# Seven block products for all six token blocks: the second MLP's first product in a fused attention and two-MLP kernel

## The chip, the cores and the metric

The kernel runs on one core of a Trainium2 chip. The metric is the device time of one execution in microseconds (us). Three runs of the kernel before took 1200.7, 1200.85 and 1199.98 us; their median is 1200.7 us.

## The reference

Three layers follow each other on 3072 tokens of 512 values. Attention runs over chunks of 32 tokens with 16 tokens of context to the left, 8 to the right and 8 memory tokens. The first MLP has a width of 1536, the second one of 2048. The change lies in the second:

```python
def _moe2_ref(x, w_in, w_out):
    h = x @ w_in                                  # 3072 x 512 times 512 x 2048
    g = h * (1.0 / (1.0 + np.exp(-1.702 * h)))
    return (g @ w_out).astype(np.float32)         # 3072 x 2048 times 2048 x 512
```

All inputs are 64-bit floats in DRAM. The kernel turns each weight block of 128 x 512 into two tiles of 32-bit floats, a high part and a low part (the rest), and it makes one product of two such numbers out of three matmuls: high by high, high by low, low by high.

## The kernel before

**Order of the work.** The code does not write instructions directly. Every step is handed to `add(engine, cost, function, reads, writes)` of the class `Schedule`. At the end `run` goes through the steps with the estimated costs and starts on each engine the ready step with the earliest due time. The due times come from TensorE's products, whose sum of costs is the variable `clock[0]`. What comes out is one fixed list per engine (TensorE or PE, VectorE or DVE, ScalarE or ACT, GpSimd or POOL, and SyncE or SP, which issues DMAs). On the chip each engine goes through its list in order, and an instruction that waits holds all those behind it on its engine.

**First MLP.** The tokens are six blocks of 512. For each block, `first_product` makes 12 column blocks of each of the two inner products (12 matmuls of 128x512 for each, 8 on line 740 and 4 on line 747). `gated` makes the gate: ScalarE's tanh on line 764, VectorE's product on line 767, then the high part on ScalarE (line 772) and the low part on VectorE (line 775). `gemm2` adds the outer product into the four banks Y (line 918). The result of a block is copied out of Y by ScalarE (line 938) and stored in DRAM as `y_dram`, transposed.

**Conversion of weights.** `convert` loads a block of 64-bit floats into one of three tiles `raw` (line 254) and turns it into 32-bit floats in one of two tiles `f`: ScalarE shifts the exponent (line 258), VectorE shifts the low words (line 263), VectorE (line 272) or, every second time, ScalarE (line 268) isolates the sign, and VectorE joins the parts (line 277). Then ScalarE writes the high part into a weight slot (line 282), and VectorE, or every third time GpSimd, writes the low part (line 287). The 16 blocks of `w2_in` and the 16 of `w2_out` go through this in turn while the last block of the first MLP and the first of the second run; the slots are those of the first MLP's 36 weight blocks, in the order in which these have been used up (`freed`).

**Second MLP, tokens 0 to 1023.** Here two blocks of 512 tokens are done plainly (`for b in range(NBP)`): `y_in` loads a block of y and splits it into high and low parts (GpSimd makes the low ones, line 964); for each of 16 column blocks `first_product` issues 12 matmuls, `gated` makes the gate, and `gemm4` adds the outer product (12 matmuls, line 716).

**Second MLP, tokens 1024 to 3071.** These are two superblocks of two blocks each. A superblock goes through 8 pairs of column blocks (`NPR`). For a pair, the product of a 2 x 2 block matrix of weights with a 2 x 2 block matrix of tokens is made by the scheme of Strassen and Winograd: seven block products (`part_product`, 6 matmuls each, line 1247) instead of eight. The sums and differences of the tokens' blocks are made by `x_prep`, once a superblock, and of the weights' blocks by `combine(j)`, once for all: it rebuilds pair j from the slots, makes four sums, splits them and stores all seven operands in DRAM (`wc_dram`). `fetch` brings them back, a pair at a time, into a ring of 14 operands in 7 tiles `sb_r`. Around the block products ScalarE copies a bank three times a pair (`snap`, line 1259), VectorE adds a bank to such a copy three times (`plus`, line 1263), and four gates are made (`gate2`, lines 1290 and 1293). Two of the four are outer-multiplied at once: `gemm4` of the pair ahead stands among the block products. The other two wait in tiles `gbs` for the superblock's second half, which is 16 times `gemm4`.

```python
SEQ = ["m1", "m5", "m6", "m2", "m3", "m7", "m4"]
...
part_product(g, "m7", a, False)
plus("s5", a)
gate2(lambda: work["s5"], "s5", 2 * j + 1)
if fill:
    gemm4(*fill.pop(0))
part_product(g, "m4", a, False, ...)
```

`m4` adds to the bank that `plus("s5", a)` reads; between them TensorE has one `gemm4`.

## Time and profile before

| | before |
|---|---|
| median of three runs | 1200.7 us (1199.98 to 1200.85) |
| the profiled execution | 1197.44 us |
| its span, first to last instruction | 1195.7 us |
| instructions in the trace | 19083 |
| mean granted clock of TensorE | 0.994 |
| GpSimd busy | 82.1 us |
| DMA traffic | 122.08 MB, mean 102 GB/s |

The profile comes from one execution, which took 1197.44 us; the span is 1.7 us shorter. The page cuts the span into 40 slices of some 30 us: attention and the first MLP fill slices 1 to 23, the two plain blocks of the second MLP go from about 700 to 863 us, and the superblocks follow from there. Busy time counts an instruction from its start to its end; instructions of one engine overlap, so the time from one start to the next can be shorter than the length of one.

### The profile page before, as it was taken

Reading aid. Unit: us, or ns where it says so; the run is one execution under the profiler, and the core shown is the slowest. Engines: PE = TensorE matmul, PEld = TensorE weight load, DVE = VectorE, ACT = ScalarE, POOL = GpSimd, SP = SyncE. Lnnn points to the kernel's source line nnn. Section 1 sums busy time; section 2 is a strip of 40 time slices with the busy share of each in tenths; the row PEclk is TensorE's granted clock in tenths of the full one; section 3 lists DMA queues with packets and bytes.
Section 4 is the critical chain, followed back from the end, with each engine's and each line's share of the span. In section 5 each row is a group of like instructions: output and inputs, shape, how many; then the busy total and the mean of one; then the engine's idle time right before and its main releaser. Section 6 shows DMA issues by size and latency. Waiting matters only on the chain.

```text
span 1195.7 us, 19083 instructions
## 1 busy us (share of the span) xinstructions
PE 1173.8 (98%) x7352; PEld 980.1 (82%) x7352; DVE 712.5 (60%) x1454; ACT 455.6 (38%) x794; POOL 82.1 (7%) x80
## 2 busy tenths in 40 slices
PE   5899999999999999999999999999999999999998
PEld 4788899988888888888878888888888888888887
DVE  7899857783687158518877734666243357253342
ACT  5588722222222122212467742334233344243332
POOL 2221210000000000000111120000000000000000
PEclk9799999999999999999999999999999999999999
DMA  9466333233132112301377722235244443244101
GB/s 222 140 193 199 102 81 56 52 53 75 32 52 51 45 29 52 82 10 26 122 223 241 231 89 71 88 123 185 79 141 124 123 144 120 63 131 115 44 36 36
DMA packets 200779, 122.08 MB, mean 102 GB/s; under 512 B 138608, under 2 KB 173680, under 8 KB 200688
## 3 DMA queue, kind: packets, MB, share of 16 engines
q1 hardware_dynamic: 197232, 114.56, 35.2%
q10 hardware_dynamic: 3456, 6.29, 1.4%
q8 instruction: 58, 0.95, 0.3%
q14 instruction: 33, 0.27, 0.1%
HBM read 93.54 MB, written 27.26 MB: 101 GB/s over the span
## 4 chain that ended last, share of the span: by engine, by line
PE 93%; DVE 3%; DMA 2%; SPq 1%; ACT 1%; issue 0%; DVEq 0%; ACTq 0%
PE bank L740 25%; PE bank L716 22%; PE bank L918 15%; PE bank L747 13%; PE bank L1247 13%; PE bank L652 2%; PE bank L502 2%; SPq L307 1%; PE bank L592 1%; DMA raw<-in_moe_w_out_dram 1%; DVE pw L570 0%; DMA raw<-in_moe_w_in_dram 0%; DVE raw L272 0%; PE bank L393 0%; DMA y_dram<-f 0%
## 5 line engine op out<-in xcount | busy, mean ns | idle before, releaser
L740 PE MATMUL bank<-xh,w 128*128 128x512 f32 (+1 forms) x784 | 284.3, 369 | 3.3 <-ACT w L282 1.6
L740 PE MATMUL bank<-xl,w 128*128 128x512 f32 (+1 forms) x784 | 282.8, 368 | 0.0
L716 PE MATMUL bank<-w,gh 128*128 128x512 f32 x768 | 236.5, 389 | 0.0
L747 PE MATMUL bank<-xh,w 128*128 128x512 f32 (+1 forms) x784 | 192.2, 370 | 0.0
L740 PEld LDWEIGHTS bank<-xh,w 128*128 128x128 f32 x784 | 147.7, 188 | 30.1 <-ACT w L282 2.4
L716 PEld LDWEIGHTS bank<-w,gh 128*128 128x128 f32 x768 | 144.2, 188 | 29.9
L740 PEld LDWEIGHTS bank<-xl,w 128*128 128x128 f32 x784 | 147.9, 189 | 24.2
L767 DVE SCALAR_TENSOR_TENSOR sig<-sig,bank 128x512 f32<-128x512 f32 (+1 forms) x114 | 72.9, 639 | 158.0 <-PE bank L747 99.0
L747 PEld LDWEIGHTS bank<-xh,w 128*128 128x128 f32 x784 | 138.2, 189 | 25.1
L918 PE MATMUL bank<-gh,w 128*128 128x512 f32 (+1 forms) x656 | 158.2, 364 | 0.0
L716 PE MATMUL bank<-w,gl 128*128 128x512 f32 x384 | 149.5, 389 | 0.0
L764 ACT ACTIVATE sig<-bank 128x512 f32<-128x512 f32 (+1 forms) x114 | 63.8, 560 | 196.6 <-PE bank L747 189.1
L772 ACT ACTIVATE gh<-sig 128x512 fp32r<-128x512 f32 (+1 forms) x114 | 67.8, 595 | 181.6 <-DVE sig L767 166.4
L918 PEld LDWEIGHTS bank<-gh,w 128*128 128x128 f32 x656 | 114.8, 189 | 19.5
L1247 PE MATMUL bank<-sb_x,sb_r 128*128 128x512 f32 x480 | 115.9, 389 | 0.0
L1247 PEld LDWEIGHTS bank<-sb_x,sb_r 128*128 128x128 f32 x480 | 90.1, 188 | 18.7
L775 DVE SCALAR_TENSOR_TENSOR gl<-sig,gh 128x512 fp32r<-128x512 f32 (+1 forms) x114 | 73.9, 648 | 42.1 <-ACT gh L772 39.7
L716 PEld LDWEIGHTS bank<-w,gl 128*128 128x128 f32 x384 | 72.1, 188 | 15.0
L627 DVE STREAM_TRANSPOSE pt<-raw 32x256 f32<-32x256 f32 x184 | 80.0, 435 | 2.4
L918 PE MATMUL bank<-gl,w 128*128 128x512 f32 (+1 forms) x328 | 80.7, 368 | 0.0
L1263 DVE TENSOR_TENSOR sb_s<-bank,sb_s 128x512 f32<-128x512 f32 x48 | 33.1, 691 | 68.9 <-PE bank L1247 58.2
L918 PEld LDWEIGHTS bank<-gl,w 128*128 128x128 f32 x328 | 56.7, 189 | 9.8
(123 smaller groups left out, 1171.7 us busy)
## 6 DMA issues: line engine op xcount, KB each, us to landing
sb_r<-wc_dram SPq DMA_DIRECT2D x112, 256.0 KB
raw<-in_moe_w_out_dram SPq DMA_DIRECT2D x24, 512.0 KB
raw<-in_moe_w_in_dram SPq DMA_DIRECT2D x16, 512.0 KB
y_dram<-f ACTq DMA_DIRECT2D x24, 256.0 KB
wc_dram<-w SPq DMA_DIRECT2D x24, 256.0 KB
out_dram<-f SPq DMA_DIRECT2D x23, 256.0 KB
vn<-in_v_dram SPq DMA_DIRECT2D x24, 240.0 KB
f<-in_q_dram SPq DMA_DIRECT2D x276, 16.0 KB
```

The source lines that it names most:

```text
L502: nc.tensor.matmul(bk[c * CH : (c + 1) * CH, p * KW : (p + 1) * KW], T["qt"][r, p, c * CH : (c + 1) * CH], T["kt"][r, p, c, :], start=True ...
L627: nc.vector.transpose(T["pt"][r * CH : (r + 1) * CH, :, c * CH : (c + 1) * CH], T["pn"][c * CH : (c + 1) * CH, :, kb * CH : (kb + 1) * CH],)
L716: nc.tensor.matmul(ps_out, a, c, start=(first and i == 0 and j == 0), stop=(last and i == n - 1 and j == 2),)
L740: nc.tensor.matmul(bank[bk][:, :n], w[:, 0, ts[t]], x[xb][:, t, c0 : c0 + n], start=t == 0 and x is xhs, stop=False)
L747: nc.tensor.matmul(bank[bk][:, :n], w[:, 1, ts[t]], xhs[xb][:, t, c0 : c0 + n], start=False, stop=t == NK - 1)
L764: nc.scalar.activation(sig[:, :n], bank[src_sig][:, :n], AF.Tanh, scale=scale / 2)
L767: nc.vector.scalar_tensor_tensor(out=sig[:, :n], in0=sig[:, :n], scalar=1.0, in1=bank[src_val][:, :n], op0=ALU.add, op1=ALU.mult)
L772: nc.scalar.activation(gh[:, :n], sig[:, :n], AF.Copy, scale=0.5)
L775: nc.vector.scalar_tensor_tensor(out=gl[:, :n], in0=sig[:, :n], scalar=0.5, in1=gh[:, :n].bitcast(F32), op0=ALU.mult, op1=ALU.subtract)
L918: nc.tensor.matmul(bank[Y[m]][:, c0 : c0 + n], w[:, wi, m * P : (m + 1) * P], g[:, :n], start=f == 0 and j == 0 and c0 == 0, stop=f == F1 ...
L1247: nc.tensor.matmul(bank[bk], w[:, o : o + P], xt[x, k][:, xl, :], start=first and k == 0 and wl == 0 and xl == 0, stop=k == 1 and wl == 1, ...
L1263: nc.vector.tensor_tensor(out=work[n], in0=bank[bk], in1=work[n], op=ALU.add)
```

## The change

The plain blocks are taken out, and three superblocks cover all the tokens. The main parts of the diff:

```diff
-    NBP = 2
-    NSB = (NB2 - NBP) // 2
+    NSB = NB // 2
...
-    def y_in(b, xb):
...
-    def combine(j):
...
+    def produce(j):
+        pair = [convert(None, cols(w2_in, 2 * j + i), put=True) for i in range(2)]
+        (wa, ka), (wb, kb) = pair
...
+            def hi():
+                nc.scalar.activation(part(0), src(), AF.Copy)
+            def lo():
+                nc.vector.tensor_tensor(out=part(1), in0=src(), in1=part(0).bitcast(F32), op=ALU.subtract)
+            def store():
...
+                    out=wc_dram[d : d + n].rearrange("m p c -> p m c"), in_=w()[:, o : o + n, :].bitcast(F32)
...
+            add("act", c_act(n * H2), hi, r=ks, w=ring)
+            add("dve", c_dve(n * H2), lo, r=ks, w=ring)
+            add("sp", 0.45, store, r=ring, w=[("wc", j, m) for m in ms], nbytes=n * P * 512 * 4)
...
+        cut((MA11, MA12), two(lambda: wa), [ka])
+        sub(lo_, lambda: wb[:, lo_], lambda: wb[:, hi_], [kb], ALU.add)
+        sub(hi_, t(lo_), lambda: wa[:, lo_], [tl, ka])
+        cut((MS1, MS2), two(lambda: work["t"]), [tl, th])
+        sub(lo_, lambda: wa[:, hi_], t(hi_), [th, ka])
+        sub(hi_, lambda: wa[:, lo_], lambda: wb[:, lo_], [ka, kb])
+        cut((MS4, MS3), two(lambda: work["t"]), [tl, th])
+        cut((MA22,), lambda: wb[:, hi_].rearrange("p (m c) -> p m c", m=1), [kb])
...
-    CW0 = 6
-    pend = None
-    nh = 0
-    for b in range(NBP):
...
+    produce(0)
+    produce(1)
+    x_prep(0)
...
+    for f in range(F2):
+        convert(slot_out2[f], rows(w2_out, f))
+    fill = [lambda: gemm2(*last1)]
...
+            if j + 2 < NPR and sb == 0:
+                produce(j + 2)
+            elif g + 2 < NSB * NPR:
+                if g + 2 == NPR:
+                    add("none", 0.0, open_raw, w=conv_keys + KYS + [("gB", 14), ("gB", 15)])
                 fetch(g + 2)
```

`convert` stops after the join when it is called with `put`. `produce(j)` makes the seven operands of pair j straight from the two joined blocks, in the ring's tiles, and stores them for the superblocks that follow. Pairs 0 and 1, the tokens' sums of superblock 0 and all of `w2_out` stand ahead of or at the start of superblock 0; pair j + 2 is produced while pair j runs. `x_prep(0)` works in the tiles of the first MLP's token block 4. The last `gemm2` of the first MLP becomes the filler of pair 0.

Three places show what moved; the names are tiles with numbers that tell them apart, `bank_66` to `bank_73` being the eight banks.

TensorE at the passage from the first MLP to the second, before (`w_1608` is the first MLP's last weight block; the rows from 740 on are the second MLP's first column blocks):

```order
L747 MATMUL bank_67<-xh_88,w_102 128x512 x4
L918 MATMUL bank_70<-gl_87,w_1608 128x512
L918 MATMUL bank_73<-gl_87,w_1608 128x512
L740 MATMUL bank_66<-xh_88,w_104 128x512
L740 MATMUL bank_66<-xl_89,w_104 128x512
L747 MATMUL bank_66<-xh_88,w_104 128x512 x4
L747 MATMUL bank_67<-xh_88,w_106 128x512 x4
L716 MATMUL bank_70<-w_101,gh_84 128x512 x2
```

and with the change:

```order
L920 MATMUL bank_73<-gl_86,w_1607 128x512
L1227 MATMUL bank_69<-sb_x_6197,sb_r_6014 128x512 x3
L1227 MATMUL bank_68<-sb_x_6276,sb_r_6014 128x512 x3
L1227 MATMUL bank_66<-sb_x_6229,sb_r_5992 128x512 x3
L1227 MATMUL bank_68<-sb_x_6337,sb_r_6053 128x512 x3
L920 MATMUL bank_70<-gh_85,w_1608 128x512
L1227 MATMUL bank_67<-sb_x_6190,sb_r_6139 128x512 x3
L920 MATMUL bank_70<-gl_87,w_1608 128x512
L1227 MATMUL bank_69<-sb_x_6197,sb_r_6092 128x512 x3
L718 MATMUL bank_70<-w_645,gh_84 128x512 x2
```

The block products (line 1227 now) begin ahead of the first MLP's last two `gemm2`, and 30 of them stand between its last matmul and the first `gemm4` (line 718), where before 24 matmuls of the plain product stood.

VectorE in the second MLP's first steps, before (lines 263, 272, 277 and 287 are conversions, 767 and 775 the gate):

```order
L263 TENSOR_SCALAR raw_75<-raw_75 128x512
L775 SCALAR_TENSOR_TENSOR gl_87<-sig_83,gh_85 128x512
L287 TENSOR_TENSOR w_654<-f_77,w_654 128x512
L277 SCALAR_TENSOR_TENSOR f_78<-f_78,raw_75 128x512
L767 SCALAR_TENSOR_TENSOR sig_82<-sig_82,bank_66 128x512
```

and with the change in pair 1 of superblock 0 (line 1243 is `plus`, 1273 and 1257 the gates, 1174 a weight sum, 1192 a low part of operands):

```order
L1243 TENSOR_TENSOR sb_s_5943<-bank_66,sb_s_5943 128x512
L1174 TENSOR_TENSOR sb_t<-f_78 128x256
L1243 TENSOR_TENSOR sb_s_5945<-bank_67,sb_s_5945 128x512
L1192 TENSOR_TENSOR sb_r_5992<-f_77,sb_r_5992 128x2x256
L1174 TENSOR_TENSOR sb_t<-sb_t,f_77 128x256
L1273 SCALAR_TENSOR_TENSOR sig_82<-sig_82,sb_s_5943 128x512
L1243 TENSOR_TENSOR sb_s_5944<-bank_69,sb_s_5944 128x512
L1192 TENSOR_TENSOR sb_r_6014<-sb_t,sb_r_6014 128x2x256
L1257 SCALAR_TENSOR_TENSOR gl_86<-sig_82,gh_84 128x512
```

All conversions and operands of pairs 2 to 7 now stand between the sums and gates of superblock 0 on the same engine; `w2_out` is converted ahead of them, the last two blocks in pair 0.

TensorE near the start of the first MLP's last block, before (bank 67 takes the second inner product, and line 767 on VectorE has to read it before it is written again):

```order
L747 MATMUL bank_67<-xh_749,w_103 128x512 x4
L747 MATMUL bank_66<-xh_749,w_105 128x512 x4
L740 MATMUL bank_67<-xh_749,w_106 128x512
L740 MATMUL bank_67<-xl_750,w_106 128x512
L918 MATMUL bank_70<-gh_84,w_104 128x512
```

and with the change:

```order
L749 MATMUL bank_67<-xh_749,w_103 128x512 x4
L749 MATMUL bank_66<-xh_749,w_105 128x512 x4
L920 MATMUL bank_70<-gh_84,w_104 128x512
L742 MATMUL bank_67<-xh_749,w_106 128x512
L742 MATMUL bank_67<-xl_750,w_106 128x512
```

Four matmuls of the outer product now stand ahead of the one that reuses bank 67.

## Rows read from the trace of the kernel before

**Rows 1.** The page, busy time by engine and the chain that ended last.

```profile
PE 1173.8 (98%) x7352; PEld 980.1 (82%) x7352; DVE 712.5 (60%) x1454; ACT 455.6 (38%) x794; POOL 82.1 (7%) x80
...
PE 93%; DVE 3%; DMA 2%; SPq 1%; ACT 1%; issue 0%; DVEq 0%; ACTq 0%
```

**Rows 2.** Who waited for whom, TensorE alone, from 588 us to the end.

```profile
PE bank L740 <- DVE sig L767: 0.9, 1, 0.9
```

**Rows 3.** The timeline of TensorE; start, length (us), line, tiles, count.

```profile
700.27 1.98 PE L747 MATMUL bank<-xh,w 128*128 128x512 f32 x8
702.08 0.62 PE L716 MATMUL bank<-w,gh 128*128 128x512 f32 x2
...
895.20 5.60 PE L1247 MATMUL bank<-sb_x,sb_r 128*128 128x512 f32 x24
900.64 0.62 PE L716 MATMUL bank<-w,gh 128*128 128x512 f32 x2
```

**Rows 4.** Busy time in two stretches: PE, PEld, DVE, ACT, POOL, clock, DMA, GB/s.

```profile
606.00:650.00 44.00, 43.25 (x191) 35.83 (x192) 33.63 (x55) 30.18 (x46) 5.31 (x4) 1.00 0.73 232
...
863.00:960.00 97.00, 97.00 (x429) 80.36 (x428) 40.27 (x62) 35.57 (x60) 0.00 (x0) 1.00 0.44 128
```

**Rows 5.** The timeline of VectorE in the seven-product stage.

```profile
913.08 0.69 DVE L1263 TENSOR_TENSOR sb_s<-bank,sb_s 128x512 f32<-128x512 f32 x1 [4.96 <-PE bank L1247]
...
915.80 0.69 DVE L1263 TENSOR_TENSOR sb_s<-bank,sb_s 128x512 f32<-128x512 f32 x1
916.41 0.68 DVE L1293 SCALAR_TENSOR_TENSOR sb_g<-sig,sb_s 128x512 f32<-128x512 f32 x1
...
928.04 0.69 DVE L1263 TENSOR_TENSOR sb_s<-bank,sb_s 128x512 f32<-128x512 f32 x1 [4.96 <-PE bank L1247]
```

**Rows 6.** The timeline of VectorE, sums of 256 columns.

```profile
752.53 0.42 DVE L1105 TENSOR_TENSOR cw_s<-cw_b 128x256 f32<-128x256 f32 x1
752.87 0.42 DVE L1106 TENSOR_TENSOR cw_s<-cw_a,cw_b 128x256 f32<-128x256 f32 x1
```

**Rows 7.** Groups by line and shape: VectorE, 600 to 700 us; ScalarE, 860 to 960.

```profile
L277 DVE SCALAR_TENSOR_TENSOR f<-f,raw 128x512 int32<-128x512 int32 x29 | 20.6, 721 | 6.4 <-ACT f L258 6.0
L287 DVE TENSOR_TENSOR w<-f,w 128x512 fp32r<-128x512 f32 x20 | 15.6, 784 | 3.6 <-ACT w L282 3.6
L263 DVE TENSOR_SCALAR raw<-raw 128x512 int32<-128x512 int32 x28 | 15.0, 540 | 5.5 <-DMA raw<-in_moe_w_in_dram 4.4 <-DMA raw<-in_moe_w_out_dram 1.0
L272 DVE TENSOR_SCALAR raw<-raw 128x512 uint16<-128x512 uint16 x14 | 11.7, 833 | 0.2
...
L1259 ACT ACTIVATE sb_s<-bank 128x512 f32<-128x512 f32 x18 | 10.8, 598 | 26.0 <-PE bank L1247 26.0
```

**Rows 8.** Issue of a load by SyncE, and the VectorE instruction that waited for it.

```profile
632.30 0.38 SPq L254 DMA_DIRECT2D raw<-in_moe_w_in_dram  x1
...
636.38 0.43 DVE L263 TENSOR_SCALAR raw<-raw 128x512 int32<-128x512 int32 x1 [1.17 <-DMA raw<-in_moe_w_in_dram]
```

**Rows 9.** The timeline of TensorE about its one wait.

```profile
603.87 1.98 PE L747 MATMUL bank<-xh,w 128*128 128x512 f32 x8
606.75 0.50 PE L740 MATMUL bank<-xh,w 128*128 128x512 f32 x1 [0.91 <-DVE sig L767]
```

**Rows 10.** The timelines of VectorE and ScalarE ahead of that wait.

```profile
602.74 0.46 DVE L263 TENSOR_SCALAR raw<-raw 128x512 int32<-128x512 int32 x1
605.07 0.69 DVE L277 SCALAR_TENSOR_TENSOR f<-f,raw 128x512 int32<-128x512 int32 x1 [1.87 <-ACT f L258]
...
606.01 0.68 DVE L767 SCALAR_TENSOR_TENSOR sig<-sig,bank 128x512 f32<-128x512 f32 x1
...
603.23 1.37 ACT L268 ACTIVATE raw<-raw 128x512 f16<-128x512 f32 x1 [1.92 <-DVE raw L263]
```

**Rows 11.** Busy time in a stretch of the start, columns as in rows 4.

```profile
30.00:40.00 10.00, 7.94 (x60) 6.74 (x61) 9.01 (x19) 3.85 (x8) 3.15 (x3) 0.50 0.09 32
```

More of the change, by code (lines that the diff above doesn't have):

```diff
@@ L227, with convert @@
     sraw = []
-    def convert(slot, src, gate=None):
+    def convert(slot, src, gate=None, put=None):
         u = nconv[0]
@@ L297, in convert @@
             add("act", 1.4, sign, r=[kr], w=[kr2])
-        add("dve", 0.7, join, r=[kr, kr2], w=[kf])
+        add("dve", 0.7 if u < NW else 0.75, join, r=[kr, kr2], w=[kf])
+        if put:
+            return ft, kf
         add("act", c_act(512), high, r=[kf] + gate, w=[("w", slot, 0)])
@@ L993 @@
             pend = (b, f, i, m, c0)
-    gemm2(*pend)
+    last1 = pend
     step_ns[0] = 32 / 2400.0
@@ L1009, with gemm4 @@
     add("none", 0.0, lambda: None, w=done + conv_keys)
-    slot_in2 = [freed[2 * f][1] for f in range(F2)]
-    slot_out2 = [freed[2 * f + 1][1] for f in range(F2)]
-    rest2 = [s for _, s in freed[2 * F2 :]]
-    for f in range(F2):
-        convert(slot_in2[f], cols(w2_in, f))
-        convert(slot_out2[f], rows(w2_out, f))
-    def gemm4(f, i, banks, row, end=False, mark=None):
+    def gemm4(f, i, banks, row, end=False):
         gh, gl = ghs[i], gls[i]
@@ L1031, in gemm4 @@
             [("w", s, 0), ("w", s, 1), ("gh", i), ("gl", i)],
-            [("bank", k) for k in banks] + ([mark] if mark else []),
+            [("bank", k) for k in banks],
         )
@@ L1140 @@
+    ids = [s for _, s in freed]
+    NRH = 14
+    ring_at, x_at, out_at = ids[: NRH // 2], ids[NRH // 2 : NRH // 2 + 14], ids[NRH // 2 + 14 :]
+    slot_out2 = out_at[:-1] + ["o0", "o1"]
+    assert len(slot_out2) == F2
     xt, ringh, gbs, work, ys = {}, {}, {}, {}, {}
-    NRH = 14
+    ringt = [lambda i=i: ringh["t", i] for i in range(NRH // 2)]
     def open_slot_as(s, name, dtype, put_, keys):
@@ L1300, in gate2 @@
         add("dve", c_dve(BLK), mul, r=[ksrc, ks], w=[("gB", f)])
-    CW0 = 6
-    pend = None
-    nh = 0
-    for b in range(NBP):
-        xb = (NB + b) % 2
-        for f in range(F2):
-            hb = Hb[nh % 2]
-            nh += 1
-            first_product(slot_in2[f], xb, BLK, hb)
-            i, tail = gated(BLK, hb, 1.702, hb)
-            tail()
-            j, odd = divmod(b * F2 + f - CW0, 2)
-            now = not odd and 0 <= j < NPR
-            if pend:
-                gemm4(*pend, mark=("cm", j) if now else None)
-            if now:
-                combine(j)
-            if f == 0 and b + 1 < NBP:
-                y_in(b + 1, (xb + 1) % 2)
-            pend = (f, i, O[b], b * BLK)
@@ L1345 @@
-    add("none", 0.0, open_x1b, w=xkeys(1 - x0) + [("gB", f) for f in range(8, 16)])
-    sets = [[6, 7, 0, 1], [2, 3, 4, 5]]
-    assert sorted(O[NBP - 1]) == sets[1]
-    fill = [pend]
-    fetch(0)
-    fetch(1)
+        open_slot_as(sl, f"sb_r{i}", F32R, put_, [("ring", 2 * i), ("ring", 2 * i + 1)])
+    homes = [(m, k) for m in range(NMP) for k in range(2)]
+    for (m, k), sl in zip(homes, x_at):
+        open_slot_as(sl, f"sb_x{m}{k}", F32R, x_one(m, k), [("X", m, k)])
+    add("none", 0.0, open_x1, w=xkeys(1 - x0) + [("w", f"o{i}", h) for i in (0, 1) for h in (0, 1)] + [("gB", f) for f in range(8, 12)])
@@ L1355 @@
         ob = [bb, e, a0, a1]
-        row = (NBP + 2 * sb) * BLK
-        ready = []
+        row = 2 * sb * BLK
         for j in range(NPR):
@@ L1364 @@
             snap("s5", e)
-            if fill:
-                gemm4(*fill.pop(0))
+            if len(fill) > 1:
+                fill.pop(0)()
             part_product(g, "m6", a, False)
```

184 lines of the change are left out of this document (71 added, 113 removed).

## The prediction

> **What bounds the kernel now.** I read the page's first part and its chain first. TensorE is busy for 98% of the span, VectorE for 60%, and 93% of the chain that ended last is TensorE [rows 1]. A busy share alone can hide gaps, so next came the list of who waited for whom: from 588 us on, TensorE waited once, for 0.9 us [rows 2]. Third, the pace: 24 block products' matmuls start at 895.20 us and the next group at 900.64, which is 5.44 / 24 = 0.2267 us a matmul, and the plain product's eight take 702.08 - 700.27 = 1.81 us, 0.2263 each [rows 3]. Both loops run at one pace, back to back, at a granted clock of 1.00 [rows 4]. So from 588 us on the time is the number of matmuls times 0.2267 us, as long as every operand is there in time. In the superblocks the other engines have room: VectorE is busy for 40 of 97 us there, against 34 of 44 us in the stretch where weights are converted [rows 4]. The change puts these two loads side by side, and that is the question.
>
> **The change, part by part.**
>
> *Matmuls.* The plain first product of tokens 0 to 1023 is 2 blocks x 16 column blocks x 12 = 384 matmuls. A superblock has 8 pairs x 7 products x 6 = 336. The outer products stay (32 `gemm4` either way). TensorE loses 48 matmuls: 48 x 0.2267 = 10.9 us, all on the path [rows 1, 3]. The Trainium skill's page "TensorE: Matmul & The Clock Gate", section "Back-to-back issue gap", gives some 131 ns for a sustained matmul of 512 columns; by that figure the loss would be only 48 x 0.131 = 6.3 us. The rows contradict it in both loops, and the measurement decides.
>
> *VectorE beside superblock 0.* This is the unknown cost, and I make it pair by pair. A pair takes TensorE 7 x 6 + 2 x 12 = 66 matmuls, 15.0 us; in the trace the same `plus` comes again after 928.04 - 913.08 = 14.96 us [rows 5]. Pair 0 has one outer product of 12 matmuls and takes 54 x 0.2267 = 12.2 us. From the order of the change I count VectorE's rows between one pair's `plus("s1")` and the next:
>
> - pair 0: 14 of 512 columns (9 sums and gates, 3 joins, 2 low parts), 3 shifts, 2 signs
> - pair 1: 15 of 512 (9, 2 joins, 4 low parts of operands), 8 of 256, 3 shifts, 1 sign
> - pair 2: 15 of 512, 7 of 256, 3 shifts, 1 sign
> - pair 3: 15 of 512, 5 of 256, 2 shifts, 2 signs
> - pair 4: 16 of 512, 5 of 256, 1 shift
>
> after which the load falls away. An instruction of 512 columns lasts 0.69 us, but the next one starts 916.41 - 915.80 = 0.61 us after it [rows 5]; one of 256 columns lasts 0.42 and starts the next 0.34 later [rows 6]. Shifts and signs I take at their full means, 0.54 and 0.83 us [rows 7]. With the start-to-start times, pair 1 is 15 x 0.61 + 8 x 0.34 + 3 x 0.54 + 0.83 = 14.3 us, and pairs 0, 2, 3 and 4 come to 11.8, 14.0, 13.6 and 12.0. VectorE also waits for its partners: in the conversion stretch it sat idle for 6.4 + 3.6 + 5.5 + 0.2 = 15.7 us over 29 joins, 0.54 us each [rows 7]. With that (3, 2, 2, 2 and 4 joins) the five pairs take 13.4, 15.4, 15.1, 14.7 and 14.2 us against TensorE's 12.2 and four times 15.0. VectorE falls behind by at most 1.2 + 0.4 + 0.1 = 1.7 us and catches up in pairs 3 and 4.
>
> What would that lag hold up? The tightest place is `m4`, which may start only after `plus("s5")`; one `gemm4` of 12 matmuls, 2.7 us, lies between, less 0.69 us for the sum itself [rows 5]: 2.0 us of cover. So 1.7 us of lag is just hidden, and I put this term at 0. The far end uses full lengths instead of start-to-start times: 0.69 and 0.42 us. Then the pairs take 14.5, 17.3, 16.8, 16.3 and 15.9 us with the waits, the lag adds up to 2.3 + 2.3 + 1.8 + 1.3 + 0.9 = 8.6 us, and TensorE loses 8.6 - 2.0 = 6.6 us. The near end is nearer to the truth, since successive starts on this very engine are 0.61 us apart [rows 5]; a gain below 0 is excluded, as TensorE does not wait in this stage now [rows 2].
>
> *The operands themselves.* The ring holds two pairs. In the order, the low part of pair 2's first operand stands beside pair 1's `plus("s5")`, two `gemm4` and one block product (30 matmuls, 6.8 us) ahead of its use, and those of pairs 3 and 5 further ahead still. VectorE's lag of 1.7 us eats into this cover first; it gets no term of its own. ScalarE has 17 instructions a pair, and 25 in the 80 matmuls (18.1 us) in and after pair 1, where the Y banks are emptied too; at 0.60 us each [rows 7] these are 10 and 15 us.
>
> *Transfers.* A pair now loads 1 MB of weights and stores 1.75 MB of operands in 15 us, 184 GB/s; the conversion stretch moves 232 [rows 4]. There a load took 636.38 - 632.30 = 4.1 us from its issue to the instruction that waited for it, and VectorE waited 1.17 us of that [rows 8]. On SyncE's queue a pair's two loads stand behind the stores of the pair before, and these wait for VectorE's low parts, so a late low part delays the loads, and a shift that waits for a load holds VectorE's list. That is what the 0.54 us a join stands for. In DRAM, pairs' operands are stored once and fetched for two superblocks, 112 fetches as before: nothing.
>
> *The passage between the MLPs.* The Y banks must be copied out before the first `gemm4`. Between the last `gemm2` and it stood 24 matmuls (5.4 us) and no wait [rows 2]; now there are 30 (6.8 us). Nothing.
>
> *The one wait of before.* TensorE's last start ahead of it is due at 603.87 + 8 x 0.2267 = 605.68, and the next comes at 606.75 [rows 9]. VectorE's product of the gate stood behind a join that waited 1.87 us for ScalarE, which had itself waited 1.92 us for a shift on VectorE [rows 10]. With the change TensorE has four other matmuls there, but they need banks that ScalarE has to empty in the same tangle. I take 0; the ends are 0.9 gained and 0.9 lost.
>
> **The sum.** 1197.4 - 10.9 = 1186.5 us for an execution like the profiled one (span 1195.7). The median of the runs shown lies 3.3 us higher; against it the forecast is 1200.7 - 10.9 = **1189.8 us**. About 0.2% (2.4 us) is what a measurement of this kernel can tell from no change.
>
> **The rivals.**
>
> *VectorE gives part of it back* (chance 0.22). The far end above: 1189.8 + 6.6 = 1196.4 us. For it: pairs 0 to 3 fill VectorE's time, and one tangle such as that before the wait costs a microsecond [rows 9, 10]. Against it: the start-to-start times, which are measured on this engine [rows 5, 6].
>
> *The production chain decides: slower* (0.05). A pair has only two tiles `f`, so the chain of one pair (shift exponents, join, four sums, four splits back and forth between ScalarE and VectorE) must end before the next begins. At 0.6 to 0.7 us a step, 15 steps are about 10 us; if a load of 4.1 us [rows 8] and a sign of 0.83 us [rows 7] lie bare in it, 15; each of the waits of 1.9 us that the trace shows [rows 10] comes on top. At two a pair it would be 18.8 us, and six pairs would lose 6 x 3.8 = 22.8, less the pair of lead that the ring gives, 15.0: 7.8, still faster. It is slower than before when a pair takes over 15.0 + (10.9 + 15.0) / 6 = 19.3 us; at 20 us the loss is 6 x 5.0 - 15.0 = 15.0 and the time 1189.8 + 15.0 = 1204.8 us. Against it: the third tile `raw` lets loads run ahead.
>
> *TensorE's clock falls* (0.02). From 30 to 40 us, after a stretch in which TensorE had long gaps, its granted clock was 0.50, the 1.2 GHz level, while in the stretch with the 0.9 us wait it was 1.00 [rows 11, 4]. Should waits bunch in superblock 0, one pair at half clock would cost a further 15.0 us: with the 6.6 us, 1189.8 + 21.6 = 1211.4 us. The same page of the Trainium skill, section "What's actually happening", says that the gate follows how busy the array has been; by that rule waits cost twice, and the stretch at the start agrees [rows 11].
>
> *The gain is hidden* (0.05). Superblock 0 would start about 10 us late, because its sums of tokens or first operands are not ready: some 1200 us. Against it: in the order the last split of tokens stands on VectorE four steps of the first MLP, some 33 us, ahead of the first block product.
>
> **How the numbers follow.** Forecast 0.66, part given back 0.22, hidden 0.05, chain 0.05, clock 0.02. The first two are faster by over 0.2% (the second's end, 1196.4, lies under 1198.3): 0.88. Same: 0.05. Slower: 0.07. The range goes down to 1186.5 (the wait of before gone, and an execution as quick as the profiled one) and up to 1196.5, the far end for VectorE, which leaves out the last three cases.
>
> **What would show it.** Right: 7304 matmuls; no wait of TensorE over 1 us in superblock 0; `plus("s5")` ending before the `gemm4` beside it; VectorE nine tenths busy there. Wrong: block products of line 1227 that wait for VectorE's `plus` or for the ring, pair after pair, or a clock under 1.00 there.

## The result and the profile after

The changed kernel takes 1187.31 us (median of 4 runs, 1185.67 to 1189.07) against 1200.34 us for the kernel before on the same chip (4 runs, 1198.01 to 1200.85). The ratio is 0.9895, 95% interval 0.9874 to 0.9917: 13.0 us faster, by the interval 10 to 15, which holds the 10.9 us of the forecast too. The forecast was 1189.8 us, range 1186.5 to 1196.5. The profiled execution took 1185.67 us with a span of 1183.9; that of before had 1197.44 and 1195.7, so profile against profile it is 11.8 us.

The page of the changed kernel, busy time by engine, the chain that ended last, and the group of the block products, which answer to [rows 1]:

```profile
PE 1162.3 (98%) x7304; PEld 970.8 (82%) x7304; DVE 724.4 (61%) x1489; ACT 471.8 (40%) x832; POOL 64.2 (5%) x67
...
PE 96%; DVE 3%; ACT 1%; issue 0%; DMA 0%; POOL 0%; DVEq 0%; SPq 0%; ACTq 0%
...
L1227 PE MATMUL bank<-sb_x,sb_r 128*128 128x512 f32 x1008 | 241.0, 389 | 0.0
```

TensorE has 7304 matmuls where it had 7352, and lost 11.5 us of busy time. VectorE gained 35 instructions and 11.9 us; TensorE's block products waited for none of it ("0.0" behind the bar).

The stretches of the changed kernel in which VectorE makes block operands beside tokens 0 to 1023 (busy us of PE, PEld, DVE, ACT, POOL with counts, clock, DMA share, GB/s):

```profile
706.00:721.00 15.00, 15.00 (x68) 12.43 (x67) 13.34 (x26) 10.46 (x19) 0.00 (x0) 1.00 0.77 263
721.00:736.00 15.00, 15.00 (x68) 12.43 (x67) 12.65 (x26) 9.91 (x17) 0.00 (x0) 1.00 0.74 243
736.00:751.00 15.00, 15.00 (x68) 12.42 (x67) 13.16 (x27) 10.73 (x17) 0.00 (x0) 1.00 0.64 222
751.00:766.00 15.00, 15.00 (x68) 12.40 (x67) 12.74 (x25) 11.08 (x19) 0.00 (x0) 1.00 0.55 201
```

Each line is about one pair. TensorE is full in all of them at a granted clock of 1.00, VectorE busy for 12.7 to 13.3 us of 15. From 588 us to the end, the view of who waited for whom has no row for TensorE. The one that stood there before [rows 2] is gone, as TensorE's timeline at that place shows:

```profile
604.15 1.98 PE L749 MATMUL bank<-xh,w 128*128 128x512 f32 x8
605.96 1.07 PE L920 MATMUL bank<-gh,w 128*128 128x512 f32 x4
```

Eight matmuls at 0.2267 us fill the time up to 605.96, where before a hole of 0.91 us stood [rows 9].

**One measure for all that follows.** The first 600 us of a program vary by some 2 us from execution to execution, whatever the kernel (those eight matmuls start between 603.9 and 606.2 us in the profiles below). So I compare kernels by their profiles from the start of these eight matmuls to the start of the last matmul, and call it the tail. Before: 603.87 to 1191.50, 587.63 us. After: 604.15 to 1179.73, 575.58 us. The tail fell by 12.05 us: 10.88 are the 48 matmuls, 0.91 the wait that is gone, and of the last 0.26 some 0.14 lie in the eight matmuls behind that wait, which took 1.95 us (606.75 to 608.70) in place of 1.81.

### The profile page after: what moved, and what is told of

Read it like the earlier page. It is cut to its first block, busy times and chain, and to the rows that moved or that the text cites. A ratio compares the mean times of both kernels' runs of the same rounds, so it can differ in the third digit from the quotient of the medians.

```text
span 1183.9 us, 19055 instructions
## 1 busy us (share of the span) xinstructions
PE 1162.3 (98%) x7304; PEld 970.8 (82%) x7304; DVE 724.4 (61%) x1489; ACT 471.8 (40%) x832; POOL 64.2 (5%) x67
## 4 chain that ended last, share of the span: by engine, by line
PE 96%; DVE 3%; ACT 1%; issue 0%; DMA 0%; POOL 0%; DVEq 0%; SPq 0%; ACTq 0%
PE bank L718 22%; PE bank L742 22%; PE bank L1227 19%; PE bank L920 17%; PE bank L749 11%; PE bank L654 2%; PE bank L504 2%; PE bank L594 1%; DVE pw L572 1%; PE bank L395 0%; DMA qn<-in_q_dram 0%; DVE sm L561 0%; DVE mx L521 0%; DVE e L524 0%; PE bank L387 0%
## 5 line engine op out<-in xcount | busy, mean ns | idle before, releaser
L1227 PE MATMUL bank<-sb_x,sb_r 128*128 128x512 f32 x1008 | 241.0, 389 | 0.0
L742 PE MATMUL bank<-xh,w 128*128 128x512 f32 (+1 forms) x656 | 234.1, 365 | 2.8 <-ACT w L282 2.1
L742 PE MATMUL bank<-xl,w 128*128 128x512 f32 (+1 forms) x656 | 233.0, 363 | 0.0
L1227 PEld LDWEIGHTS bank<-sb_x,sb_r 128*128 128x128 f32 x1008 | 189.2, 188 | 39.3
L718 PE MATMUL bank<-w,gh 128*128 128x512 f32 x672 | 207.0, 389 | 0.0
L749 PE MATMUL bank<-xh,w 128*128 128x512 f32 (+1 forms) x656 | 158.2, 366 | 0.0
L742 PEld LDWEIGHTS bank<-xh,w 128*128 128x128 f32 x656 | 123.7, 189 | 23.7 <-ACT w L282 2.3
L742 PEld LDWEIGHTS bank<-xl,w 128*128 128x128 f32 x656 | 123.8, 189 | 19.4
L749 PEld LDWEIGHTS bank<-xh,w 128*128 128x128 f32 x656 | 114.1, 189 | 20.1
L769 DVE SCALAR_TENSOR_TENSOR sig<-sig,bank 128x512 f32<-128x512 f32 (+1 forms) x82 | 50.9, 620 | 104.3 <-PE bank L749 103.7
L1239 ACT ACTIVATE sb_s<-bank 128x512 f32<-128x512 f32 x72 | 43.1, 599 | 68.8 <-PE bank L1227 64.8
L1270 ACT ACTIVATE sig<-sb_s 128x512 f32<-128x512 f32 x72 | 45.5, 632 | 58.6 <-DVE sb_s L1243 37.2
```

Source lines behind the costliest of these rows:

```text
L718: nc.tensor.matmul(ps_out, a, c, start=(first and i == 0 and j == 0), stop=(last and i == n - 1 and j == 2),)
L742: nc.tensor.matmul(bank[bk][:, :n], w[:, 0, ts[t]], x[xb][:, t, c0 : c0 + n], start=t == 0 and x is xhs, stop=False)
L749: nc.tensor.matmul(bank[bk][:, :n], w[:, 1, ts[t]], xhs[xb][:, t, c0 : c0 + n], start=False, stop=t == NK - 1)
L769: nc.vector.scalar_tensor_tensor(out=sig[:, :n], in0=sig[:, :n], scalar=1.0, in1=bank[src_val][:, :n], op0=ALU.add, op1=ALU.mult)
L1227: nc.tensor.matmul(bank[bk], w[:, o : o + P], xt[x, k][:, xl, :], start=first and k == 0 and wl == 0 and xl == 0, stop=k == 1 and wl == 1, ...
L1239: add("act", c_act(BLK), lambda: nc.scalar.activation(work[n], bank[bk], AF.Copy), r=[("bank", bk)], w=[n])
```

## The experiments

Three things were open: whether the 10.9 us are all of the gain and all TensorE's, how much room VectorE has left beside superblock 0, and where the one wait of before came from. "Superblock 0" is tokens 0 to 1023.

### The 48 matmuls put back

```diff
             part_product(g, "m1", a, True)
+            if sb == 0:
+                part_product(g, "m1", a, True)
```

> The changed kernel with the product m1 made twice in each of the eight column pairs of tokens 0 to 1023 (the second starts its bank anew, so what is computed stays the same): the 48 matmuls that the change took away are back, and nothing else of the change is undone. Theory: TensorE is the only bound there, a matmul of 128x512 costs its pace of 0.2267 us (row group 3), so the run is 48 x 0.2267 = 10.9 us slower than the changed kernel, 1198 us (10.4 to 11.4 slower, profile against profile). Rival: VectorE sets part of the pace there, the added matmuls then run in time in which TensorE waited, and the run is less than 9 us slower. By the figure of 131 ns for a matmul in the Trainium skill, page TensorE: Matmul & The Clock Gate, section Back-to-back issue gap, it would be 48 x 0.131 = 6.3 us, an estimate.

Measured: median 1197.11 us; tail 586.45 us (604.58 to 1191.03), 10.87 us above the changed kernel, and no wait of TensorE.

```profile
689.35 8.32 PE L1227 MATMUL bank<-sb_x,sb_r 128*128 128x512 f32 x36
697.51 1.07 PE L920 MATMUL bank<-gh,w 128*128 128x512 f32 x4
```

This is TensorE's timeline in that run; where the changed kernel has 30 block products in a row, 36 stand here, and they take 8.16 us, 0.2267 each. 10.87 / 48 = 0.2265 us: the theory holds to 0.01 us (48 x 0.2267 = 10.88), the rival falls. So does the price of 131 ns in the Trainium skill, page "TensorE: Matmul & The Clock Gate", section "Back-to-back issue gap": it would have made 6.3 us.

The run says one thing more. It has as many matmuls as the kernel before, 7352, and all the rest of the change, and it is still faster than the kernel before on the same chip: 1197.11 against 1199.92 us (11 and 15 runs, ratio 0.9980, interval 0.9971 to 0.9989). So 2.8 us of the gain, in medians, are not the matmuls. In the profiles the two tails differ at one place only, the wait of the kernel before and the matmuls right behind it; what the first 600 us add to the medians is not known.

### Operands not made at all

```diff
             if j + 2 < NPR and sb == 0:
-                produce(j + 2)
+                pass
```

(and the ring and the fetches take the operands of pairs 0 and 1 again)

> The changed kernel without the making of the operands of column pairs 2 to 7: pairs 2 to 7 are multiplied with those of pairs 0 and 1 again (so the output is wrong), in both superblocks; VectorE loses about 8 us of work a pair in tokens 0 to 1023, ScalarE 5, and the loads of the second MLP's first weight fall away but for two pairs. TensorE's matmuls are the same in number. Theory: VectorE, ScalarE and the transfers cost nothing there, so no change (-0.5 to +0.5 us profile against profile from 590 us on, 1187 us). Rival: part of the gain was still given back beside them, 1 to 4 us, and this run is that much faster, 1183 to 1186 us.

Measured: median 1187.24 us; tail 575.58 us (605.01 to 1180.59), the same to the hundredth of a microsecond as with all operands made. VectorE's busy time from 588 to 800 us fell from 152.20 to 117.03 us and the transfers' rate from 175 to 93 GB/s. Nothing of the gain was given back beside VectorE, ScalarE or the transfers; the first rival of the prediction, in its mild form too, falls.

### VectorE in another order

```diff
-        add("dve", 0.42 if u < NW else 0.55, rest, r=[kr], w=[kr2])
+        add("dve", 0.42, rest, r=[kr], w=[kr2])
...
-        add("dve", 0.7 if u < NW else 0.75, join, r=[kr, kr2], w=[kf])
+        add("dve", 0.7, join, r=[kr, kr2], w=[kf])
```

> The changed kernel with the scheduler's costs for the shift and the join of the second MLP's weights put back to those of the kernel before (0.42 and 0.7): the same instructions, VectorE's in another order in tokens 0 to 1023. Theory: since VectorE has 2 us of a pair's 15 to spare, its order matters little: 0 to 1 us slower, 1187 to 1188 us. Rival: the gain hangs on that order; TensorE then waits for VectorE in most of eight pairs and the run is 2 to 8 us slower.

Measured: median 1187.79 us; tail 575.58 us (606.21 to 1181.79), no wait. The cost numbers in the change are worth nothing by themselves: the room that VectorE has covers either order.

### Less TensorE work per pair: how much room is left

```diff
-            part_product(g, "m4", a, False, ("p2", sb) if j == NPR - 1 else None)
+            if sb > 0:
+                part_product(g, "m4", a, False, ("p2", sb) if j == NPR - 1 else None)
```

> The changed kernel without the product m4 in the eight column pairs of tokens 0 to 1023: that part of the result is wrong, since one of the seven products is left out; 48 matmuls fewer. It asks how much cover VectorE has left. Theory from the trace of the changed kernel (VectorE busy 12.7 to 13.2 us of each 15 us between 721 and 766 us): a pair falls from 15.0 to 13.6 us of TensorE, still over 13.2, so the run gains 9 to 10.9 us, about 1177 us. Rival, the VectorE durations of my forecast (13.4 to 15.4 us a pair): TensorE then waits for VectorE in nearly all pairs that make operands, and the run gains 1 to 5 us only, 1182 to 1186 us.

Measured: median 1175.87 us; tail 564.85 us (605.14 to 1169.99), 10.73 less than the changed kernel. But m4 is also the place where a lag of VectorE would show, so the run took the meter away with the work. The next one leaves out m3 instead:

```diff
-            part_product(g, "m3", e, False)
+            if sb > 0:
+                part_product(g, "m3", e, False)
```

> The changed kernel without the product m3 in the eight column pairs of tokens 0 to 1023 (that part of the output leaves out one of the seven products); m4, before which TensorE can wait for VectorE's reading of a bank, stays. 48 matmuls fewer, and a pair of TensorE falls by 1.36 us to 13.6. It repeats the question of the run without m4 in a place where a lag of VectorE must show, since there the wait itself was left out with the product. Theory, from the run with the sums made twice (1.36 us more of VectorE a pair cost 1.65 us in all): the gain is 10.9 less 1 to 3 us of new waits in front of m4, so 8 to 10 us, about 1178 us. Rival: VectorE has more than 1.4 us of cover in every pair and the loss there was something else; the gain is 10.7 to 10.9 us, 1176.5 us, with no wait. Second rival, the VectorE durations of my forecast: a gain of 1 to 5 us.

Measured: median 1175.24 us; tail 564.70 us (604.00 to 1168.70), 10.88 less, which is all of 48 x 0.2267, and no wait of TensorE. The rival I had put against my own theory holds: VectorE has at least 1.36 us of room in every pair. Tokens 0 to 1023 would still be TensorE's with one product in seven fewer.

### More VectorE work per pair

```diff
             def fn():
-                nc.vector.tensor_tensor(out=work["t"][:, o], in0=x(), in1=y(), op=op)
+                for _ in range(2):
+                    nc.vector.tensor_tensor(out=work["t"][:, o], in0=x(), in1=y(), op=op)
```

> The changed kernel with each of the four sums of 256 columns that VectorE makes for a column pair made twice (same output, same order of everything else): 4 x 0.34 = 1.36 us more of VectorE in each of six pairs of tokens 0 to 1023. Theory from the trace of the changed kernel: 12.7 to 13.2 us of VectorE a pair become 14.0 to 14.6, still under 15.0, so no change (0 to 1 us slower, 1187 to 1188 us). Rival, the VectorE durations of my forecast (13.4, 15.4, 15.1, 14.7 and 14.2 us in the first five pairs): they become 14.8 to 16.8, and the run is 3 to 6 us slower, 1190 to 1193 us.

Measured: median 1189.54 us; tail 577.23 us (605.60 to 1182.83), 1.65 us longer. That is between the two expectations, and at odds with the room of 1.36 us that the run without m3 shows. The row of TensorE's only listed wait in that run, and VectorE's timeline ahead of it:

```profile
PE bank L1228 <- DVE sb_s L1244: 0.8, 1, 0.8
```

```profile
725.18 0.68 DVE L1193 TENSOR_TENSOR sb_r<-sb_t,sb_r 128x512 fp32r<-128x512 f32 x1
728.46 0.43 DVE L263 TENSOR_SCALAR raw<-raw 128x512 int32<-128x512 int32 x1 [2.60 <-DMA raw<-in_moe_w_in_dram]
728.80 0.68 DVE L1244 TENSOR_TENSOR sb_s<-bank,sb_s 128x512 f32<-128x512 f32 x1
```

VectorE was not short of time there: it stood idle for 2.60 us in front of a shift whose load had not landed, and the sums that free TensorE's banks (L1244) stood behind that shift. SyncE's queue, with its DMA issues, first in the changed kernel and then with the sums made twice:

```profile
709.48 7.42 SPq L1196 DMA_DIRECT2D wc_dram<-sb_r  x4
717.21 3.08 SPq L254 DMA_DIRECT2D raw<-in_moe_w_in_dram  x2
```

```profile
710.93 8.80 SPq L1197 DMA_DIRECT2D wc_dram<-sb_r  x4
720.04 2.04 SPq L254 DMA_DIRECT2D raw<-in_moe_w_in_dram  x2
```

The loads (L254) come behind four stores of operands, each of which waits for a low part from VectorE. Counted from the eight matmuls (604.15 and 605.60), the first store is issued at 105.33 us in both, the loads at 113.06 and 114.44: 1.38 us later, a pair's added work. VectorE came to the shift at 728.46 - 2.60 - 605.60 = 120.26 us, as early as in the changed kernel, where it ran at 120.18 without a wait; it then stood until 122.86. So the added work did not stop VectorE where it was done, but through its load. At most 1.38 us of that wait come from the later issue; the other 1.3 us or so are a load that was also slower to land, and why stays open. No run moved the loads ahead of the stores, so this path is read from the trace and not tested. Of the 1.65 us the list shows 0.8, a start 0.23 us late at 746.05 is too little for it, and the rest is spread over still smaller ones.

The same, with each sum made four times:

> As the run with the sums made twice, but each of the four sums made four times: 12 x 0.34 = 4.1 us more of VectorE in each of six pairs. Theory from the trace of the changed kernel: a pair of VectorE takes 16.8 to 17.3 us against 15.0 of TensorE; of the 6 x 4.1 = 24.5 us added, some 14 us lie in VectorE's idle time of the six pairs, so 6 to 10 us slower, 1193 to 1197 us, with TensorE's waits on banks read by VectorE. Rival, the VectorE durations of my forecast: 13 to 16 us slower, 1200 to 1203 us. If VectorE bounded nothing at all, no change.

Measured: median 1206.88 us, 6.5 us above the kernel before (ratio 1.0053, interval 1.0040 to 1.0065); tail 595.85 us, 20.3 above the changed kernel and over both expectations. TensorE's waits in that run:

```profile
PE bank L1228 <- DVE sb_s L1244: 9.4, 3, 4.3
PE bank L1228 <- ACT sb_s L1240: 4.6, 2, 4.3
```

and the stretches behind the longest of them (columns as above):

```profile
730.00:740.00 10.00, 5.70 (x19) 4.27 (x18) 8.12 (x18) 4.63 (x8) 0.00 (x0) 0.83 0.39 148
750.00:760.00 10.00, 6.37 (x22) 4.86 (x21) 9.82 (x20) 5.28 (x10) 0.00 (x0) 0.83 0.29 106
780.00:790.00 10.00, 5.73 (x25) 4.41 (x24) 8.93 (x20) 5.73 (x9) 0.00 (x0) 0.98 0.36 139
790.00:800.00 10.00, 10.00 (x39) 8.13 (x38) 9.60 (x20) 4.44 (x8) 0.00 (x0) 0.85 0.25 95
```

The waits are 14.0 us. The granted clock (behind the counts) stands at 0.83, 0.83, 0.98 and 0.85 around the waits of 4.30, 3.63 and 4.27 us; taken as shares of 10 us each that is about another 1.7 + 1.7 + 0.2 + 1.5 = 5.1 us. Both together make 19.1 of the 20.3. VectorE itself waited for 3.6 us in all between 700 and 800 us, 1.68 of them for a load (ahead of 732.95), so most of TensorE's waits is VectorE's own added work here. That holds also where TensorE waits for ScalarE's copy (the 4.27 us), since ScalarE had itself waited 3.19 us for VectorE's sums. My expectation had counted VectorE's idle time as room to the last microsecond (14 of the 24.5 us added) and had no term for the clock.

### GpSimd at work beside VectorE

```diff
+    def beside(j):
+        def fn():
+            t = ringh[place(j + 2, MA11)].bitcast(F32)[:, :384]
+            nc.gpsimd.tensor_tensor(out=work["q"], in0=t, in1=t, op=ALU.subtract)
+
+        for _ in range(8):
+            add("pool", c_pool(384), fn, r=[("ring", place(j + 2, MA11))], w=["qq"])
...
                 produce(j + 2)
+                beside(j)
```

> The changed kernel with GpSimd at work beside VectorE in tokens 0 to 1023: behind each of six column pairs' operands, GpSimd makes eight idle subtractions of 384 columns into a buffer that nothing reads (48 in all; the output stays the same). In the kernel before, shifts of VectorE lasted 540 ns and signs 833 ns over a stretch in which GpSimd worked, and one sign 1.84 us beside a GpSimd subtraction; in the changed kernel shifts of that kind last 421 ns beside an idle GpSimd. Theory: GpSimd beside is what stretched them. Then here the shifts' mean between 706 and 780 us rises from 421 to over 500 ns and the signs' from 752 to over 1000 ns, and the time by 0 to 4 us (1187 to 1191 us). Rival: their durations come from the order of VectorE's own instructions; they stay at 421 and 752 ns, and the time stays.

Measured: median 1201.51 us, level with the kernel before (ratio 1.0006, interval 0.9997 to 1.0014); tail 590.22 us, 14.6 above the changed kernel. The theory on the durations held, its price did not. VectorE's groups between 706 and 790 us, shifts, sums of 256 columns and sums from a bank, first with GpSimd idle (the changed kernel), then with GpSimd beside:

```profile
L1243 DVE TENSOR_TENSOR sb_s<-bank,sb_s 128x512 f32<-128x512 f32 x18 | 12.3, 688 | 9.1 <-PE bank L1227 8.3 <-ACT sig L1270 0.7
...
L263 DVE TENSOR_SCALAR raw<-raw 128x512 int32<-128x512 int32 x9 | 3.8, 421 | 0.0
...
L1174 DVE TENSOR_TENSOR sb_t<-f,f 128x256 f32<-128x256 f32 x6 | 2.5, 419 | 0.0
```

```profile
L1252 DVE TENSOR_TENSOR sb_s<-bank,sb_s 128x512 f32<-128x512 f32 x15 | 10.1, 683 | 0.7 <-PE bank L1236 0.7
...
L263 DVE TENSOR_SCALAR raw<-raw 128x512 int32<-128x512 int32 x9 | 7.2, 804 | 3.5 <-DMA raw<-in_moe_w_in_dram 3.5
L1183 DVE TENSOR_TENSOR sb_t<-f,f 128x256 f32<-128x256 f32 x5 | 4.5, 895 | 0.0
```

Shifts go from 421 to 804 ns, these sums from 419 to 895 and signs (L272) from 750 to 1064; sums that take one operand from a bank stay, at 688 and 683. How they are stretched is in the two engines' timelines:

```profile
725.03 1.05 DVE L1201 TENSOR_TENSOR sb_r<-f,sb_r 128x256 fp32r<-128x256 f32 x1
726.00 1.04 DVE L1183 TENSOR_TENSOR sb_t<-sb_t,f 128x256 f32<-128x256 f32 x1
726.96 1.05 DVE L263 TENSOR_SCALAR raw<-raw 128x512 int32<-128x512 int32 x1
727.93 0.68 DVE L1252 TENSOR_TENSOR sb_s<-bank,sb_s 128x512 f32<-128x512 f32 x1
```

```profile
724.91 7.72 POOL L1171 TENSOR_TENSOR sb_q<-sb_r 128x384 f32<-128x384 f32 x8 [4.84 <-DVE sb_r L1201]
```

GpSimd's eight subtractions take 7.72 / 8 = 0.97 us each, and VectorE's three instructions start 0.97 and 0.96 us apart: one of VectorE to each of GpSimd. The Trainium skill, page "SBUF — State Buffer", section "Who interferes with whom", says that a VectorE instruction with two inputs in SBUF or in a two-port mode, and a GpSimd instruction that reads SBUF, lock each other out for a whole instruction; the rows agree. The time follows as in the run before: waits of 4.75, 1.50, 1.10 and 2.32 us make 9.7, and around the longest two the granted clock is 0.66 and 0.83 over 10 us. Not all of that fall costs time, since part of it lies inside the wait of 4.75 us itself, where TensorE has nothing to do (the stretch up to the wait's end, and the one behind it):

```profile
732.51:734.77 2.26, 0.00 (x0) 0.00 (x0) 2.26 (x5) 1.16 (x2) 0.13 (x1) 0.50 0.15 56
734.77:739.34 4.57, 4.57 (x11) 3.60 (x12) 4.57 (x9) 2.79 (x6) 0.00 (x0) 0.50 0.15 56
```

Counted from the starts of the matmuls, each against 0.2267 us, the slow ones behind the waits cost 4.2 us; with the waits that is 13.8 of the 14.6 us. The shift at 732.31 us had waited 3.07 us for its load, as with the sums made twice.

### Part of VectorE's work given to GpSimd

```diff
-                nc.vector.tensor_tensor(out=part(1), in0=src(), in1=part(0).bitcast(F32), op=ALU.subtract)
+                eng = nc.gpsimd if j > 1 and MS4 in ms else nc.vector
+                eng.tensor_tensor(out=part(1), in0=src(), in1=part(0).bitcast(F32), op=ALU.subtract)
```

(its cost entry follows)

> The changed kernel with the low part of one double operand (S4 and S3, 2 x 256 columns) of each of the column pairs 2 to 7 made on GpSimd instead of VectorE: VectorE has one subtraction of 512 columns less in six pairs (0.61 us each), GpSimd one of some 1.3 to 1.8 us. Theory, from the run with GpSimd at work beside: VectorE's subtractions and shifts beside it last about twice as long, so what GpSimd takes over VectorE loses again; no gain, 0 to 2 us slower (1187 to 1189 us), and some sums or shifts last over 600 ns. Rival: GpSimd relieves VectorE; the mean durations stay, VectorE's busy time between 706 and 781 us falls by some 3 us, and the time stays, since TensorE has no wait to lose.

Measured: median 1186.79 us; tail 575.57 us (605.11 to 1180.68), no wait. The stretch from 706 to 781 us, the changed kernel first:

```profile
706.00:781.00 75.00, 75.00 (x333) 62.10 (x332) 62.38 (x117) 49.95 (x85) 0.00 (x0) 1.00 0.64 221
```

```profile
706.00:781.00 75.00, 75.00 (x332) 62.10 (x331) 62.34 (x112) 50.90 (x87) 7.61 (x6) 1.00 0.60 208
```

VectorE ran 5 instructions fewer (six subtractions less, and one gate's low part more that falls into this stretch) and was busy as long as before, 62.34 against 62.38 us: its shifts took 656 ns in place of 421 and its joins 790 in place of 684. Of the 4.1 us of the six subtractions, shifts and joins took back 2.1 + 1.3; for 7.61 us of its own work GpSimd relieved VectorE of next to nothing. The time stays, as both theories had it, since TensorE has no wait to lose.

### The one wait of the kernel before

In the profile of before, a sign on VectorE at 601.10 us, just ahead of [rows 10], lasted 1.84 us beside a GpSimd subtraction (600.54, 1.80 us). So I first took GpSimd for the cause of the wait.

```diff
-            eng = nc.vector if low_dve else nc.gpsimd
+            eng = nc.vector if low_dve or u >= NW else nc.gpsimd
...
-                nc.gpsimd.tensor_tensor(
+                nc.vector.tensor_tensor(
                     out=xls[xb][:, m, :], in0=st[:, :BLK], in1=xhs[xb][:, m, :].bitcast(F32), op=ALU.subtract
```

> The kernel before with GpSimd's low parts of the second MLP's weights and of its inputs made on VectorE instead, in the same place of the order: 8 low parts of inputs and some 10 of weights. TensorE's order is the same. It asks where the single wait of 0.9 us in front of the second MLP came from. Theory: the sign that VectorE made there lasted 1.84 us because GpSimd worked beside it; here it lasts about 0.8 us, the wait of TensorE at 606 us is gone, and the run is about 0.9 us faster from 590 us on (1199.4 us). Rival: the order of VectorE's work makes the wait; it stays (0.9 us) or grows by the added work.

Measured: median 1197.72 us against 1200.38 for the kernel before on the same chip (8 and 18 runs, ratio 0.9978, interval 0.9968 to 0.9988), 2.7 us faster; tail 586.69 us (604.88 to 1191.57), 0.94 below before, and the wait is gone from the view. That looked like the theory, though 2.7 us are three times the 0.9 that it forecast. But TensorE also came 1.0 us later to that place in this execution, so two more runs followed: one with the first half of the edit alone, and the kernel before once more.

> The kernel before with the low parts of the second MLP's weights that GpSimd makes moved to VectorE, and the inputs' low parts left on GpSimd: the narrower half of the run with both moved. It asks again for the single wait of 0.9 us, counted from the plain product's eight matmuls in front of it, so that a later start of TensorE does not blur it. Theory: the sign of 1.84 us was stretched by GpSimd's weight part; it lasts 0.75 us here, VectorE's gate product starts about 1.2 us after those eight matmuls begin instead of 2.14, and TensorE's wait is under 0.2 us. Rival: the wait depended on how early TensorE came in that one execution; then it is there again whenever the eight matmuls begin near 603.9 us, and the gate product starts near 606.0 us in any case.

Measured: one time of 1198.3 us; tail 587.47 us (604.86 to 1192.33). The sign lasts 0.75 us, and yet TensorE waits:

```profile
PE bank L740 <- DVE sig L767: 0.7, 1, 0.7
```

> The kernel before, unchanged, profiled once more: does its wait of 0.9 us come back? Theory (GpSimd stretches the sign): the sign lasts about 1.8 us again and the wait is 0.7 to 1.1 us, whether the eight matmuls in front of it begin at 603.9 or at 605 us. Rival (the wait hangs on TensorE's start in that execution): a start 1 us later takes the wait away, with the sign still long.

Measured: one time of 1201.01 us; tail 590.77 us (604.26 to 1195.03), 3.14 above the other profile of the same kernel. TensorE's timeline:

```profile
604.26 1.98 PE L747 MATMUL bank<-xh,w 128*128 128x512 f32 x8
608.66 0.50 PE L740 MATMUL bank<-xh,w 128*128 128x512 f32 x1 [2.43 <-DVE sig L767]
...
609.38 0.63 PE L740 MATMUL bank<-xh,w 128*128 128x512 f32 x1
...
611.94 1.33 PE L918 MATMUL bank<-gh,w 128*128 128x512 f32 x4
```

and VectorE's ahead of it:

```profile
603.04 0.74 DVE L272 TENSOR_SCALAR raw<-raw 128x512 uint16<-128x512 uint16 x1
...
605.89 0.69 DVE L277 SCALAR_TENSOR_TENSOR f<-f,raw 128x512 int32<-128x512 int32 x1 [1.86 <-ACT f L258]
607.59 0.43 DVE L263 TENSOR_SCALAR raw<-raw 128x512 int32<-128x512 int32 x1 [1.00 <-DMA raw<-in_moe_w_in_dram]
607.93 0.68 DVE L767 SCALAR_TENSOR_TENSOR sig<-sig,bank 128x512 f32<-128x512 f32 x1
```

Here the sign lasts 0.74 us and the wait is 2.43: a long sign is not what makes the wait, and the theory falls as I had put it. GpSimd is not cleared by that. In this profile its subtraction lies beside the shift two instructions ahead of the sign:

```profile
601.18 1.33 DVE L263 TENSOR_SCALAR raw<-raw 128x512 int32<-128x512 int32 x1 [1.10 <-DMA raw<-in_moe_w_in_dram]
600.93 1.30 POOL L287 TENSOR_TENSOR w<-f,w 128x512 fp32r<-128x512 f32 x1 [1.40 <-PE bank L747]
```

The shift's successor starts 1.26 us after it, where 0.34 is the pace, so VectorE's chain came some 0.9 us later; in the first profile the sign's successor came 1.64 us after it in place of 0.53, 1.1 later. Both profiles of before have that delay, on different instructions. The two edited runs do not settle it: the one that kept a wait put 0.64 us of VectorE's own low part (602.99) into the same chain, and in the one that lost it, which moved the inputs' low parts too, VectorE also had its load earlier (the shift at 599.89 starts 4.99 us ahead of the eight matmuls, against 3.71, 3.08 and 3.35 in the three others).

The wait is also dearer than its own length: behind it six matmuls take 611.94 - 609.38 = 2.56 us, 0.43 each, at a granted clock of 0.50, the 1.2 GHz level:

```profile
609.38:611.94 2.56, 2.56 (x7) 2.00 (x6) 2.03 (x4) 1.80 (x4) 0.13 (x1) 0.50 0.79 302
```

The tail grew by 1.6 us more than the wait did (3.14 against 2.43 - 0.91 = 1.52). What all four profiles of that order share is the gate's product (L767) queued behind a join that waits 1.86 to 1.88 us for ScalarE; but one of the four has no wait, so this alone does not make it. What varies is GpSimd's work beside the chain and the load of the shift behind the join, for which VectorE waited 1.00 us here and not at all in the other profile of before. How much is GpSimd, how much the load and how much the chain between the two engines was not taken apart.

What in the change took the wait away was not isolated either, since three things changed there. VectorE has another order: the product of the gate at 605.25 us now waits for TensorE, 2.09 us. TensorE has four other matmuls (0.91 us) ahead of the one that reuses the bank. And GpSimd, busy for 5.70 us between 590 and 611 us before, has no instruction there. In none of the ten profiles of the changed kernel and its variants above does TensorE wait at this place.

## Why the prediction was right

- **48 matmuls x 0.2267 = 10.9 us.** Right: 10.87 us put back, 10.88 (without `m3`) and 10.73 (without `m4`) taken away once more. It was read from starts of successive groups [rows 3] and not from the 389 ns that a matmul lasts in the page.
- **VectorE beside superblock 0, taken at 0.** Right, with nothing given back. The pair-by-pair sum was close in its total: the forecast's rows of pairs 1 to 4 without waits come to 14.3 + 14.0 + 13.6 + 12.0 = 53.9 us, measured are 13.34 + 12.65 + 13.16 + 12.74 = 51.9. The shifts were over-priced, at 0.54 us where they start the next 0.34 later; that mean came from a stretch with GpSimd at work [rows 7, 4], and GpSimd is idle in the new stretch. The lag of 1.7 us against 2.0 of cover was therefore too gloomy: TensorE never waited, in front of `m4` or elsewhere, and a pair shorter by 1.36 us did not make it wait either. "VectorE nine tenths busy" was 62.38 of 75 us, 83%.
- **Its far end, 6.6 us, and the rival that gives part back.** Wrong for this kernel. That VectorE can hold up TensorE there is right: 4.1 us more of VectorE a pair cost 20.3 us.
- **The clock rival.** It did not happen in the changed kernel (1.00 throughout). It happened in the runs with bunched waits, and in the kernel before itself, behind a wait of 2.43 us. The rival took a bunch of waits for its condition; one wait of 2.43 us was enough. That waits cost twice was too much: 14.0 us of waits cost about 5 us more, and 2.43 us about 1.6 more.
- **Operands, transfers, the passage between the MLPs, at nothing.** Right: without operands and with half the traffic the tail is the same, and the passage has no gap. The rate was under-priced, at 184 GB/s where 201 to 263 were moved, and cost nothing all the same.
- **The production chain and the gain hidden.** Did not happen. The chain's weak place, once VectorE had more to do, looks to be another than I named: the loads behind the stores on SyncE's queue, which the transfer paragraph had as an aside.
- **The one wait of before, taken at 0 between 0.9 gained and 0.9 lost.** This is the step that failed. It was gained, and its size was read from one execution: it is 0.91 us in one profile of the kernel before and 2.43 us, with 1.6 more at the lower clock, in another. In medians the kernel gained 13.0 us, 2.1 more than the matmuls, and the kernel with the 48 matmuls put back is 2.8 us faster than before; a wait that costs 0.9 to 4.0 us can hold both. That each timed run of before had such a wait was not seen, since only two were profiled. The measured median lies 0.8 us above the low end of the range, which took in the wait gone together with an execution as quick as the profiled one; the wait's 0.9 us alone would have ended it at 1188.9. A hint stood in the prediction's own sum: the profiled execution lay 3.3 us under the median of before, and the sum took that as an offset without a cause. The second profile is 3.57 us longer than the first, and 3.14 of that is the tail with its longer wait. What made the wait, and which part of the change removed it, stays open.

## What to carry to other kernels

Where one engine is full and unwaited for, work taken off it is worth its start-to-start pace, and work put on another is free up to the room in the stretch where it lands; measure that room from both sides, by taking work from the full engine and by adding it to the other. The room can end sooner than idle time says: here 1.36 us more a pair already cost 1.65 us, by the trace because loads stood behind stores that waited for the late engine, and the engine's next wait for such a load held up what was queued behind; and behind the longer waits (2.3 to 4.8 us here) the matmuls ran at half the clock. A wait seen in a single profile has a size of that execution only: profile the kernel twice before pricing it. And a run that puts the removed work back shows in the medians what else a change brought.

## What the runs showed of the hardware that I had not expected

An idle GpSimd was no free help here: VectorE's instructions with two inputs in SBUF, and its shifts, went in step with GpSimd's, one for one (0.97 us apart in place of 0.34), and 7.61 us of GpSimd's work left VectorE's busy time at 62.3 us with 5 instructions fewer. Sums with one operand in a bank were not touched (683 ns). And a wait of 2.43 us was followed by matmuls at 0.43 us, which cost some 1.6 us beside the wait itself.
